# A 3008-point Fourier filter and an ELU layer on one core: the transform's last products as two 64x128 tiles instead of four 64x64 tiles

## The chip, the core and the metric

The kernel runs on one core of a Trainium2 chip. The metric is device time in microseconds (us) of one execution; lower is better. A change of 0.2%, about 5 us here, is about the smallest that a measurement of this kernel can tell from none.

## The reference

```python
X = np.fft.rfft(x, axis=1)                 # x: (8, 3008, 256) float32
Y = X * (filt_r + 1j * filt_i)[None]       # filters: (1505, 256)
y = np.fft.irfft(Y, n=3008, axis=1)
h = y.reshape(24064, 256) @ w_in           # (256, 2048)
g = np.where(h > 0.0, h, np.exp(np.minimum(h, 0.0)) - 1.0)
out = g @ w_out                            # (2048, 256)
```

Everything is float32.

## The kernel before, in words

The sequence length is split as 3008 = 47 x 64, and the transform, the filter and the inverse transform are done as small matrix products over these factors, one of the eight batches after the other. The result of the inverse's first factor goes through DRAM (the tensor `yds`) and is read back by `y_read` as a tile `t` of 128 partitions by 4 indices by 256 channels. The third factor, which this change touches, is the last of the transform: `n_unit(b, m)` multiplies `t` with a table `w` of cosines and sines (`tn_read`), four indices `i` of the 24 at a time, so there are six units a batch (m = 0 to 5). The first unit of the first batch is made by another function, `n_first`, with full 128x128 tiles of weights and 128 (or 64) moving columns (line 575). That leaves 47 units of `n_unit`.

In one unit the contraction runs over 64 rows. The rows 0 to 63 hold one half of the terms and 64 to 127 the other (`HALVES`); their products go to two PSUM banks, `pse` and `pso`. The stationary operand (the weights that are loaded into TensorE) is a slice of the data `t`; the moving operand is the table, 64 columns wide, or 32 for the index i = 0. The channels are the output rows: 256 of them, as `dh` = 0, 1 of 128 each, and each 128 as `o` = 0, 64 of 64 each. ScalarE then copies both banks into `y` (line 558), VectorE makes sums from them (`n_sums`, lines 592 to 603), and the two layers follow.

The layers are done by `up_steps` (the product with `w_in`, line 624, into the banks `phs`, `pha`, `phd`) and `down_steps` (the product with `w_out`, line 707, into `po`), with the seven products of Strassen's scheme in Winograd's form for each 2 by 2 block. These are full 128x128 tiles of weights with 256 (for m = 0: 224) moving columns. ScalarE makes the ELU's exponentials (lines 635, 641, 642), VectorE the sums and maxima (lines 632, 646, 682 to 686).

Nothing is scheduled by a tool: the order is written by hand. The work is a list of 192 items (batch, m, quarter of the hidden layer), here called quads, 24 to a batch. In each quad the steps of "up" and "down" are interleaved one by one, and a plan (`at(quad, place, function, ...)`) puts the transform's pieces at five places in a quad. Each batch's transform is spread over the quads of the batch before it. Each engine works through its instructions in this order. While the first quads run, the weights are also converted from 64-bit to 32-bit numbers (the `w_...` functions).

A float32 product appears in the profile as two pairs of LDWEIGHTS (the load of weights, shown as PEld) and MATMUL (shown as PE). A unit of `n_unit` has 32 products, so 64 such pairs; they stand in groups of four tiles that occupy different quarters of the array at one time (two halves of the rows by two halves of the columns), 16 groups to a unit.

Of the kernel before, what the change touches and what calls it, by code (L numbers as in the profile page):

```python
# [26 lines left out]
P = 128  # L27
# [14 lines left out]
HALVES = slice(0, 64), slice(64, 128)  # L42
# [91 lines left out]
def order(m):  # L134

    return (1, 2, 3, 0) if m == 0 else tuple(range(4 * m, 4 * m + 4))
# [3 lines left out]
def kernel(  # L140
# [9 lines left out]
    nc = tc.nc  # L150
# [49 lines left out]
    def bank(name, shape=(P, 2, D)):  # L200
        i = banks.pop(0)
        return i, psM.tile(list(shape), FP32, tag="m%d" % i, name=name)
# [337 lines left out]
    def half(m):  # L540

        return 224 if m == 0 else 256

    def n_unit(b, m):
        t, w, h = t4s.pop((b, m)), tns.pop((b, m)), half(m)
        ps = [bank(n) for n in ("pse", "pso")]
        for q, i in enumerate(order(m)):
            n = 32 if i == 0 else 64
            for dh in range(2):
                for o in (0, 64):  # L550
                    for (_, p), r in reversed(tuple(zip(ps, HALVES))):
                        nc.tensor.matmul(p[o:o + 64, dh, ds(64 * q, n)], t[r, i - 4 * m, ds(dh * P + o, 64)],  # L552
                                         w[r, i - 4 * m, 0:n], start=True, stop=True)
        eo = []
        yset = ysets[(6 * b + m + (6 * b + m > 1)) % 2]
        for (k, p), scale, y in zip(ps, (1.0, -2.0), yset):
            y = y[:, :, 0:h]
            nc.scalar.activation(out=y, in_=p[:, :, 0:h], func=AXT.Copy, scale=scale)
            banks.append(k)
            eo.append(y)  # L560
        s = yset[2]
        ys[b, m] = dict(zip((1, 3, 5, 4, 6, 2, 7), [t[:, i] for t in eo for i in range(2)] + [s[:, i, 0:h] for i in range(3)]))
# [315 lines left out]
    with tc.manual_schedule():  # L878


        with tc.tile_pool(name="boot", bufs=1) as bp:
# [122 lines left out]
            for k in range(11):  # L1004
                nc.tensor.matmul(warm, w_in[0][:, 0, 0, :], w_in[0][:, 0:2].rearrange("p a b c -> p (a b c)"),
                                 start=True, stop=True)
# [13 lines left out]
        def at(quad, place, fn, *a):  # L1020
# [5 lines left out]
                 (0, 0, w_split, 8), (0, 0, x_load, 1, 2),  # L1026
                 (0, 3, w_float, 11, 1), (0, 3, w_sums, 5, nc.gpsimd), (0, 3, w_join, 7, 0), (0, 3, w_join, 9, 1), (0, 3, w_fetch, 15, nc.sync),
                 (1, 2, w_float, 8, 1, 0), (1, 2, y_write_first, 5, 8, 24), (1, 2, w_mult, 7, nc.vector), (1, 2, w_float, 8, 2), (1, 2, x_unit, 1, 0, 0), (1, 2, x_unit, 1, 0, 1), (1, 2, n_unit, 0, 1),
                 (1, 4, w_float, 11, 2),
                 (1, 0, w_join, 8, 0), (1, 0, x_unit, 1, 1, 0), (1, 0, x_unit, 1, 1, 1), (1, 0, f_arrange, 1, 1), (1, 0, n_sums, 0, 1, 0, 1), (1, 0, w_sums, 7, nc.gpsimd),  # L1030
# [19 lines left out]
                 (5, 0, w_join, 15, 0), (5, 0, w_join, 14, 0), (5, 0, y_read, 0, 3), (5, 0, w_join, 15, 1),  # L1050
                 (5, 3, w_mult, 15, nc.gpsimd),
                 (5, 1, c_last, 0, 0), (5, 1, w_mult, 14, nc.gpsimd), (5, 1, w_sums, 15, nc.gpsimd), (5, 1, n_unit, 0, 2),
                 (6, 2, n_sums, 0, 2, 0, 1),
                 (6, 0, n_sums, 0, 2, 2),
                 (8, 0, n_unit, 0, 3),
                 (9, 1, n_sums, 0, 3))
        for quad, place, fn, *a in early:
# [7 lines left out]
        for b in range(B):  # L1065
            t = (b - 1) * PER
            if b > 0:
                for c in range(NXC):
# [9 lines left out]
                    if nb < B:  # L1078
                        q, p = (((2, 1), (8, 1), (11, 1)) if b == 1 else XL)[c // 2]
# [92 lines left out]
```

## Time and profile before

| | before |
|---|---|
| median of 3 runs | 2549.34 us (2549.11 to 2549.7) |
| profiled execution: its own time, its span | 2550.1 us, 2548.3 us |
| TensorE products (PE) busy | 2518.0 us (99%) |
| TensorE weight loads (PEld) busy | 2151.5 us (84%) |
| VectorE (DVE) busy | 2099.9 us (82%) |
| ScalarE (ACT) busy | 1524.9 us (60%) |
| granted TensorE clock, mean | 0.997 |

The profile is of one execution; its own time is 0.03% above the median. Durations of matmuls are modelled and overlap each other, so the sum of their busy times is not the time that they take of the span; the distance from one start to the next is. In the shapes, "64*64 64x64" means weights of 64 rows and 64 columns, and 64 rows by 64 columns of moving data.

### The profile page before, as it was taken

The page shows a single profiled execution, that of the slowest core. Times are in us where ns is not written, and L with a number is a line of the kernel's source. Part 1 is how long each engine was busy: PE and PEld are TensorE (multiplying, and loading weights), DVE is VectorE, ACT ScalarE, POOL GpSimd, SP SyncE. Part 2 cuts the span into 40 slices and gives each one's busy share as a digit, 9 for nine tenths or more (in the row PEclk, how much of TensorE's full clock was granted, in tenths as well). Part 3 has the DMA queues.
Part 4 walks back from the last instruction along what each step waited for, and adds up shares of the span by engine and source line. Part 5 has one row for each costly group of instructions (what it writes and reads, how often), then busy time and mean ns, then how long its engine had stood idle before and what let it go on. Part 6 is the DMA issues. An engine that isn't in the chain of part 4 may idle for free.

```text
span 2548.3 us, 45119 instructions
## 1 busy us (share of the span) xinstructions
PE 2518.0 (99%) x17326; PEld 2151.5 (84%) x17326; DVE 2099.9 (82%) x3654; ACT 1524.9 (60%) x2702; POOL 170.4 (7%) x242
## 2 busy tenths in 40 slices
PE   8899999999999999999999999999999999999998
PEld 5688889888898888988889888888889888898887
DVE  5998888888888888788887888878898788876766
ACT  6666556655566555665566655666656665555554
POOL 3431000000000000000000000000000010000000
PEclk9999999999999999999999999999999999999999
DMA  8645214423243321433225331343314332110010
GB/s 210 197 121 124 58 41 105 108 58 71 46 104 91 70 64 42 124 81 77 45 52 139 76 67 34 78 120 80 69 21 98 86 67 59 42 40 19 20 27 17
DMA packets 227958, 194.07 MB, mean 76 GB/s; under 512 B 125493, under 2 KB 208407, under 8 KB 225007
## 3 DMA queue, kind: packets, MB, share of 16 engines
q1 hardware_dynamic: 216815, 167.35, 27.2%
q0 software_dynamic: 9776, 23.58, 4.5%
q8 instruction: 136, 2.23, 0.4%
q14 instruction: 79, 0.65, 0.1%
q10 hardware_dynamic: 1152, 0.26, 0.1%
HBM read 119.24 MB, written 74.97 MB: 76 GB/s over the span
## 4 chain that ended last, share of the span: by engine, by line
PE 93%; DVE 4%; ACT 1%; issue 1%; DMA 1%; POOL 0%; SPq 0%; DVEq 0%; POOLq 0%; ACTq 0%
PE po L707 44%; PE phs L624 25%; PE phd L624 12%; PE pha L624 6%; PE pso L552 2%; PE pf L451 1%; PE pv L517 1%; PE psa L272 1%; DVE g L646 0%; PE psa L324 0%; DVE g L632 0%; PE pse L552 0%; DMA t<-tf_t 0%; PE po L385 0%; PE po L343 0%
## 5 line engine op out<-in xcount | busy, mean ns | idle before, releaser
L707 PE MATMUL po<-g,wo 128*128 128x256 f32 (+1 forms) x5376 | 1317.5, 377 | 0.0
L707 PEld LDWEIGHTS po<-g,wo 128*128 128x128 f32 x5376 | 1012.9, 190 | 162.8 <-issue 49.2
L635 ACT ACTIVATE g<-phs 128x512 f32<-128x512 f32 (+1 forms) x576 | 338.9, 588 | 726.5 <-PE phs L624 726.5
L624 PE MATMUL phs<-y,wi 128*128 128x256 f32 (+1 forms) x2288 | 581.0, 376 | 2.1 <-ACT g L635 1.6
L642 ACT ACTIVATE e<-e 128x512 f32<-128x512 f32 (+1 forms) x768 | 477.2, 621 | 24.3
L624 PEld LDWEIGHTS phs<-y,wi 128*128 128x128 f32 x2288 | 429.2, 190 | 59.8 <-ACT g L635 4.4
L632 DVE TENSOR_TENSOR g<-phd,g 128x512 f32<-128x512 f32 (+1 forms) x384 | 259.4, 675 | 223.4 <-ACT e L642 148.8
L646 DVE SCALAR_TENSOR_TENSOR g<-e,g 128x512 f32<-128x512 f32 (+1 forms) x576 | 391.4, 679 | 0.2
L641 ACT ACTIVATE e<-g 128x512 f32<-128x512 f32 (+1 forms) x576 | 353.1, 613 | 54.0 <-DVE g L632 44.3
L646 DVE SCALAR_TENSOR_TENSOR g<-e,phs 128x512 f32<-128x512 f32 (+1 forms) x192 | 129.8, 676 | 130.5 <-ACT e L642 130.4
L624 PE MATMUL phs<-ys,wi 128*128 128x256 f32 (+1 forms) x784 | 198.0, 375 | 7.0 <-ACT g L635 5.0
L624 PE MATMUL phd<-y,wi 128*128 128x256 f32 (+1 forms) x768 | 194.1, 375 | 5.1 <-DVE g L632 5.1
L624 PE MATMUL phd<-ys,wi 128*128 128x256 f32 (+1 forms) x768 | 193.9, 375 | 1.1 <-DVE g L632 1.0
L624 PE MATMUL pha<-ys,wi 128*128 128x256 f32 (+1 forms) x752 | 190.0, 375 | 0.0
L641 ACT ACTIVATE e<-phs 128x512 f32<-128x512 f32 (+1 forms) x192 | 113.0, 589 | 114.7 <-PE phs L624 114.6
L624 PEld LDWEIGHTS phs<-ys,wi 128*128 128x128 f32 x784 | 148.0, 190 | 26.0 <-ACT g L635 6.2
L624 PEld LDWEIGHTS phd<-y,wi 128*128 128x128 f32 x768 | 145.5, 190 | 23.0 <-DVE g L632 6.7
L624 PEld LDWEIGHTS phd<-ys,wi 128*128 128x128 f32 x768 | 145.7, 190 | 18.3 <-DVE g L632 1.8
L624 PEld LDWEIGHTS pha<-ys,wi 128*128 128x128 f32 x752 | 142.8, 190 | 16.5
L632 DVE TENSOR_TENSOR g<-pha,g 128x512 f32<-128x512 f32 (+1 forms) x192 | 129.1, 673 | 22.9 <-PE pha L624 13.2
L683 DVE TENSOR_TENSOR g<-g,g 128x512 f32<-128x512 f32 (+1 forms) x192 | 132.0, 687 | 6.7
L686 DVE TENSOR_TENSOR g<-g,g 128x512 f32<-128x512 f32 (+1 forms) x192 | 131.1, 683 | 6.7
(200 smaller groups left out, 2100.5 us busy)
## 6 DMA issues: line engine op xcount, KB each, us to landing
t<-yd SPq DMA_DIRECT2D x94, 256.0 KB
z<-t SPq DMA_DIRECT2D x84, 256.0 KB
fall<-fp POOLq DMA_DIRECT2D x112, 192.0 KB, 5.1
t<-z SPq DMA_DIRECT2D x112, 192.0 KB
yd<-t SPq DMA_DIRECT2D x112, 192.0 KB
out_dram<-o SPq DMA_DIRECT2D x632, 32.0 KB
xc<-in_x_dram SPq DMA_DIRECT2D x84, 128.0 KB
xc<-in_x_dram SPq DMA_DIRECT2D x161, 64.0 KB
```

Source lines behind the costliest of these rows:

```text
L272: nc.tensor.matmul(p[32 * o:32 * o + 32, j, :], w[r, ts(o, 32)], t[r, o % 2, o // 2, :], start=True, stop=True, tile_position=(32 * a, 32 ...
L451: nc.tensor.matmul(pf[p][1][32 * a:32 * a + 32, js, :], fb[r, v, :], t2[r, js, a, :], start=True, stop=True, tile_position=(32 * p, 32 * a))
L552: nc.tensor.matmul(p[o:o + 64, dh, ds(64 * q, n)], t[r, i - 4 * m, ds(dh * P + o, 64)], w[r, i - 4 * m, 0:n], start=True, stop=True)
L624: nc.tensor.matmul(ps[:, a, 0:h], w_in[q][:, COMBO[n], a, :], y[n], start=start and a == 0, stop=True, skip_group_check=True)
L632: nc.vector.tensor_tensor(out=g[o], in0=i0, in1=i1, op=ALU.add)
L635: nc.scalar.activation(out=g[o], in_=i0, func=AXT.Copy)
L641: nc.scalar.activation(out=e, in_=src, func=AXT.Relu, scale=-1.0)
L642: nc.scalar.activation(out=e, in_=e, func=AXT.Exp, scale=-1.0)
L646: nc.vector.scalar_tensor_tensor(out=g[n], in0=es[n], scalar=1.0, in1=src, op0=ALU.subtract, op1=ALU.max)
L683: nc.vector.tensor_tensor(out=b12, in0=b22, in1=b12, op=ALU.subtract)
L686: nc.vector.tensor_tensor(out=g["t4"], in0=g["b21"], in1=g["t2"], op=ALU.subtract)
L707: nc.tensor.matmul(po[i][:, u, 0:h], w_out[q][:, COMBO[n], a, :], g[n][:, a, :], start=begin and a == 0 and n in (1, 3, 6, 4), stop=True, ...
```

## The change

The loop over `o` goes. One product takes all 128 channels of a `dh` as its output rows, with weights of 64 rows by 128 columns, and writes all 128 partitions of its bank. Two such tiles, one on the rows 0 to 63 and one on 64 to 127, stand side by side where four tiles of 64 by 64 stood. A unit has 16 products instead of 32, 32 pairs of load and matmul instead of 64, and still 16 groups. The values and their places in PSUM stay as they were, and so does every other instruction.

```diff
         for q, i in enumerate(order(m)):
             n = 32 if i == 0 else 64
             for dh in range(2):
-                for o in (0, 64):
-                    for (_, p), r in reversed(tuple(zip(ps, HALVES))):
-                        nc.tensor.matmul(p[o:o + 64, dh, ds(64 * q, n)], t[r, i - 4 * m, ds(dh * P + o, 64)],
-                                         w[r, i - 4 * m, 0:n], start=True, stop=True)
+                for (_, p), r in reversed(tuple(zip(ps, HALVES))):
+                    nc.tensor.matmul(p[:, dh, ds(64 * q, n)], t[r, i - 4 * m, ts(dh, P)], w[r, i - 4 * m, 0:n],
+                                     start=True, stop=True)
```

## Prediction

> **What bounds the kernel now.** I read the busy times and the chain of waits on the page first, and then the busy times by stage.
>
> ```profile
> span 2548.3 us, 45119 instructions
> ...
> PE 2518.0 (99%) x17326; PEld 2151.5 (84%) x17326; DVE 2099.9 (82%) x3654; ACT 1524.9 (60%) x2702; POOL 170.4 (7%) x242
> ...
> PE 93%; DVE 4%; ACT 1%; issue 1%; DMA 1%; POOL 0%; SPq 0%; DVEq 0%; POOLq 0%; ACTq 0%
> ```
>
> ```profile
> 84.00:212.00 128.00, 116.59 (x818) 99.52 (x817) 120.98 (x191) 83.24 (x151) 47.42 (x49) 0.99 0.53 140
> 212.00:2442.00 2230.00, 2229.77 (x15545) 1921.29 (x15544) 1856.92 (x3247) 1334.44 (x2359) 89.12 (x139) 1.00 0.30 70
> ```
>
> The columns of the busy times by stage are the stretch, its length, and the busy us of PE, PEld, DVE, ACT and POOL, then the granted clock. From 212 us to 2442 us TensorE is busy for 2229.77 of 2230 us, at full clock: nothing makes it wait, and what is added to or taken from its stream there is added to or taken from the time, one for one. Between 84 and 212 us, while weights are still converted, VectorE is busy for 120.98 of 128 us and TensorE has 11.4 us of gaps. A busy share of 99% doesn't say what TensorE is busy with: a product that waits for its weights counts as busy too. So the next views are the groups by shape, and one unit in order of time.
>
> ```profile
> L552 PEld LDWEIGHTS pso<-tn,t 64*64 64x64 f32 x1504 | 47.8, 134 | 15.2 <-issue 12.8 <-DVE g L685 2.3
> L272 PEld LDWEIGHTS psa<-xc,ta 32*32 32x32 f32 x1152 | 14.5, 103 | 9.0 <-issue 5.3
> L575 PEld LDWEIGHTS psn<-t,t4f 128*128 128x128 f32 x16 | 1.9, 191 | 0.9 <-DMA t4f<-yd 0.9
> ```
>
> Behind the bar stand the busy us and the mean ns of one load. A load grows with its columns: 103 ns for 32, 134 ns for 64, 191 ns for 128; the step from 64 to 128 is 57 ns. Now one unit of m = 0, first its loads, then its last products, which have 32 moving columns (start in us, duration):
>
> ```profile
> 1002.10 0.13 PEld L552 LDWEIGHTS pso<-tn,t 64*64 64x64 f32 x1 [0.33 <-DVE g L685]
> ...
> 1002.97 0.14 PEld L552 LDWEIGHTS pso<-tn,t 64*64 64x64 f32 x1
> 1002.98 0.14 PEld L552 LDWEIGHTS pse<-tn,t 64*64 64x64 f32 x1
> 1002.99 0.14 PEld L552 LDWEIGHTS pso<-tn,t 64*64 64x64 f32 x1
> 1002.99 0.14 PEld L552 LDWEIGHTS pse<-tn,t 64*64 64x64 f32 x1
> 1003.17 0.94 PEld L707 LDWEIGHTS po<-g,wo 128*128 128x128 f32 x5
> ```
>
> ```profile
> 1002.88 0.22 PE L552 MATMUL pso<-tn,t 64*64 64x32 f32 x1
> ...
> 1002.94 0.22 PE L552 MATMUL pso<-tn,t 64*64 64x32 f32 x1
> ...
> 1003.00 0.22 PE L552 MATMUL pso<-tn,t 64*64 64x32 f32 x1
> ```
>
> ```profile
> 69.85 1.86 PEld L575 LDWEIGHTS psn<-t,t4f 128*128 128x128 f32 x16 [0.94 <-DMA t4f<-yd]
> 70.40 0.75 PEld L575 LDWEIGHTS psn<-t,t4f 128*128 128x128 f32 x6
> ```
>
> The sixteenth group of loads starts 0.87 us after the first, so a group takes 0.87 / 15 = 0.058 us. Its four loads start within 20 ns and run at the same time. A stream of 64 columns takes a quarter of the 0.216 us that lies between the starts of 256-wide products, 0.054 us, and would almost explain the 0.058. The 32-wide products tell it apart: with half the stream they still start every 0.06 us. So the load of 64 columns sets the rhythm, and the stream lies beneath it. The last two lines, from `n_first`, are the nearest thing to what the change makes: loads of 128 columns with short streams behind them. Sixteen take 1.86 us, the last one 0.19 of it, so one starts every 1.67 / 15 = 0.111 us; six in the middle every (0.75 - 0.19) / 5 = 0.112 us. Four of the sixteen products have only 64 moving columns; by their streams alone, the fifteen steps would be twelve of 0.107 and three of 0.054 us, 1.45 us. They took 1.67: loads set the rhythm here too, about twice as long for twice the columns.
>
> **The change part by part.**
>
> *Removed:* half of the products of line 552, 47 x 16 = 752, that is, 1504 pairs of load and matmul. Their issue costs nothing now: the four loads of a group start 7 ns apart, and the next group's first follows about 40 ns after the fourth. What they free is not on the path.
>
> *Made longer:* each of the 16 groups of a unit now loads 128 columns instead of 64 on each half of the rows. No trace row has a load of 64 rows by 128 columns. Loads of 24x32 and 32x32 both take 103 ns, those of 48x64 133 ns against 134 ns for 64x64; fewer rows don't make a load shorter, so I take the 128x128 rhythm: 0.112 - 0.058 = 0.054 us for each group. The ends: 0.049 us (the step of a load 0.107 us, without the gap of 5 ns that the rows show) and 0.057 us (the difference of the mean durations, 191 - 134). One unit costs 16 x 0.054 = 0.864 us more. The two streams of a pair, 0.054 us, hide beneath the next load; without that cover a group would take 0.054 us more, 38 us once again; the rows of line 575, where the streams are as long or longer and still lie beneath the loads, speak against that.
>
> *Units on the path:* 44 of the 47 units start after 212 us (the first at 246 us): 44 x 0.864 = 38.0 us. The other three, at 84, 159 and 191 us, stand where TensorE has gaps of 0.7 to 3 us behind them, left by VectorE. Their 2.6 us are swallowed there, or they delay VectorE's next input and pass through. Between 0 and 2.6 I take half, 1.3 us, because in that stretch the chain of waits goes through both engines.
>
> *Entry and exit:* the first small load starts 0.31 us after the start of the last 256-wide product, where 0.216 is usual: 0.09 us lost for emptying the array. Behind the last load the next 128x128 load comes 0.18 us later, 0.07 more than the 0.11 from load to load where loads set the rhythm. Tiles that divide only the rows don't occur in the trace. The 32x32 tiles of lines 451 and 517 are entered at the same 0.31 us as the 64x64 ones, so I leave both as they are: 0. The ends: both vanish, 44 x 0.16 = -7.0 us; or emptying takes twice as long, 44 x 0.09 = +4.0 us.
>
> *Behind it:* ScalarE's copies of a unit (line 558), VectorE's sums and the next "up" steps start 0.86 us later, like TensorE's own next steps, which wait in order behind the unit. ACT has 40% idle, DVE 17% in that stage, so both keep the pace of a slower TensorE. Nothing on ACT, DVE, POOL or SP is added, taken away or moved: their streams are the same, instruction for instruction. No queue or transfer is touched.
>
> *Sum:* 38.0 + 1.3 = 39.3 us. On the profiled execution, 2550.1 + 39.3 = 2589.4 us; on the median, 0.8 us below it, 2549.3 + 39.3 = 2588.6 us, or +1.5%.
>
> **The rivals.**
>
> *First: the pair is bound by its streams, and having fewer tiles saves launches (not slower).* It holds if a load of 64x128 fits into 0.058 us, say because a tile that keeps all columns is loaded by another way than one that divides them. Then the group shrinks from 0.058 to its stream of 0.054 us: 752 x 0.004 = 3 us, 2546 us. If entry and exit vanish too, 7 us more: 2539 us. For it: no row has this shape, and four launches at 7 ns become two. Against it: the 32-wide groups that don't shrink, and the 0.112 us steps. The Trainium skill, "TensorE: Matmul & The Clock Gate", section "Measured speedup vs the span model", is on this rival's side: it gives a pack of tiles the time of one matmul plus about 4 ns for each further tile, with no term for the columns of the loads. By that rule two tiles fewer would save some 8 ns a group, an estimated 6 us in all. The trace speaks against the rule in this place: 64 and 32 moving columns give the same rhythm.
>
> *Second: the two loads of a pair don't overlap (much slower).* If two 128-column loads share a path that four 64-column loads did not need, a group takes 2 x 0.112 us: 0.166 more, 16 x 0.166 = 2.66 us a unit, 117 us for 44 units, with half of the other three 2549.3 + 117 + 4 = 2670 us. Against it: now tiles on the same columns and different rows (`pso` at 1002.97, `pse` at 1002.98) load at the same time, and the change keeps that.
>
> *Third: the program that is built still has four tiles,* and the time is 2549. The built program has 752 products fewer on TensorE, each with 128 output rows, so this is next to excluded.
>
> **How the numbers follow.** The forecast case gets 0.86: both its rhythms are measured in this trace, and what is unmeasured is only that the 128-column step holds on 64 rows. The first rival gets 0.08, of which 0.05 ends within 0.2% (5 us, about what a measurement of this kernel can tell from no change) and 0.03 below it; the second 0.05; the third 0.01. So faster 0.03, same 0.06, slower 0.91. The range is that of the forecast case with the ends of its terms. Low: the shorter step, 16 x 44 x 0.049 + 1.3 = 35.8 us, with entry and exit gone, -7.0: 28.8 us, 2578. High: the longer step in all 47 units, 47 x 16 x 0.057 = 42.9 us, or the middle sum with the doubled emptying, 39.3 + 4.0 = 43.3 us: 2593. The rivals' 0.14 lies outside.
>
> **What would show it.** Right: loads of line 551 of 64x128, half as many, near 190 ns each, in pairs every 0.112 us; a unit's loads spread over 15 x 0.112 = 1.68 us instead of 0.87; the start of the next 128x128 load 0.18 us behind the last pair; the stretch from 212 us on still without a gap of TensorE and 38 us longer; DVE and ACT busy for the same us. Wrong: pairs every 0.058 us (first rival), or single loads every 0.112 us (second); entries of other than 0.31 us; a growth between 84 and 212 us that is not between 0 and 2.6 us.

## The result, and the profile after

The changed kernel took 2589.26 us, the median of five runs (2586.39 to 2591.72), beside 2549.34 us before (2549.03 to 2549.88 in five runs): 1.0155 times the time, 95% interval 1.0143 to 1.0168. Measured once more beside other kernels, it took 2586.63 us against 2549.78 us, 1.0146 (1.0132 to 1.0160). So it is slower by 37 to 40 us; 39.3 were forecast, and the traces say below that some 37.6 is the better number.

The profiled execution took 2586.39 us. First the page's busy times and chain, then the busy times by stage (stretch, length, busy us of PE, PEld, DVE, ACT, POOL, granted clock):

```profile
span 2584.6 us, 42111 instructions
...
PE 2556.6 (99%) x15822; PEld 2191.7 (85%) x15822; DVE 2099.8 (81%) x3654; ACT 1529.7 (59%) x2702; POOL 170.4 (7%) x242
...
PE 94%; DVE 2%; DMA 2%; ACT 1%; issue 0%; SPq 0%; DVEq 0%; ACTq 0%
```

```profile
84.00:214.00 130.00, 119.93 (x749) 102.49 (x746) 121.50 (x193) 83.39 (x151) 47.49 (x49) 0.99 0.54 141
214.00:2480.00 2266.00, 2265.78 (x14157) 1957.89 (x14156) 1854.12 (x3243) 1339.62 (x2360) 89.00 (x139) 1.00 0.30 69
```

TensorE has 1504 pairs of load and product fewer and is busy longer. In the long stretch it is as full as before (2265.78 of 2266 us), and VectorE does the same work in more time. The page alone can't say more: "99%" stood there before too. The group by shape (busy us, mean ns) and the same unit as before the change, in order of time (start, duration), say it:

```profile
L551 PEld LDWEIGHTS pso<-tn,t 64*128 64x128 f32 x752 | 87.3, 188 | 15.2 <-issue 12.8 <-DVE g L684 2.3
```

```profile
1013.21 0.18 PEld L551 LDWEIGHTS pso<-tn,t 64*128 64x128 f32 x1 [0.33 <-DVE g L684]
1013.22 0.18 PEld L551 LDWEIGHTS pse<-tn,t 64*128 64x128 f32 x1
1013.32 0.19 PEld L551 LDWEIGHTS pso<-tn,t 64*128 64x128 f32 x1
...
1014.77 0.19 PEld L551 LDWEIGHTS pso<-tn,t 64*128 64x128 f32 x1
1014.78 0.19 PEld L551 LDWEIGHTS pse<-tn,t 64*128 64x128 f32 x1
1014.88 0.19 PEld L551 LDWEIGHTS pso<-tn,t 64*128 64x128 f32 x1
1014.89 0.19 PEld L551 LDWEIGHTS pse<-tn,t 64*128 64x128 f32 x1
1015.12 0.51 PEld L706 LDWEIGHTS po<-g,wo 128*128 128x128 f32 x3
```

The two loads of a pair start 7 ns apart and run together. The sixteenth pair starts 1014.88 - 1013.21 = 1.67 us after the first, so a pair follows every 1.67 / 15 = 0.111 us where a group of four followed every 0.058. The last pairs serve products with 32 moving columns and keep the same rhythm. The load is 188 ns long, like that of 128 full rows (190).

What this is worth is read between two places of the trace that are the same in both programs: the first product of the fourth unit, where TensorE's gaps end, and that of the last unit. Before, then after:

```profile
246.19 0.27 PE L552 MATMUL pso<-tn,t 64*64 64x64 f32 x1
...
2442.31 0.27 PE L552 MATMUL pso<-tn,t 64*64 64x64 f32 x1
```

```profile
245.54 0.32 PE L551 MATMUL pso<-tn,t 64*128 64x64 f32 x1
...
2477.79 0.32 PE L551 MATMUL pso<-tn,t 64*128 64x64 f32 x1
```

The distance was 2196.12 us and is 2232.25 us: 36.13 us over 43 units, 0.840 us each, and with the last unit 44 x 0.840 = 37.0 us. The stretch ahead of the fourth unit is 0.65 us shorter in this execution, so the span grew by 36.13 + 0.84 - 0.65 = 36.3 us. What the three units ahead of it add is read among the experiments.

### The profile page after: what moved, and what is told of

Its sections match the earlier page's. It is cut to its first block, busy times and chain, and to the rows that moved or that the text cites. A ratio compares the mean times of both kernels' runs of the same rounds, so it can differ in the third digit from the quotient of the medians.

```text
span 2584.6 us, 42111 instructions
## 1 busy us (share of the span) xinstructions
PE 2556.6 (99%) x15822; PEld 2191.7 (85%) x15822; DVE 2099.8 (81%) x3654; ACT 1529.7 (59%) x2702; POOL 170.4 (7%) x242
## 4 chain that ended last, share of the span: by engine, by line
PE 94%; DVE 2%; DMA 2%; ACT 1%; issue 0%; SPq 0%; DVEq 0%; ACTq 0%
PE po L706 43%; PE phs L623 25%; PE phd L623 12%; PE pha L623 6%; PE pso L551 3%; PE pf L451 1%; PE pv L517 1%; PE psa L272 1%; PE po L385 0%; DMA x<-in_x_dram 0%; PE psr L385 0%; DVE g L645 0%; DMA fall<-in_moe_w_out_dram 0%; DVE g L631 0%; DMA xc<-in_x_dram 0%
```

## The experiments

Three questions were left. Do load and stream of neighbouring groups overlap, or add up (0.054 + 0.054 us and a few ns would also make 0.112)? Is it the columns of a load that count, or that only two tiles stand abreast? And do the first three units cost anything?

**The changed kernel again, and the change in a part of the units.** The last two have this edit, with `> 3` for the 44 late units and `< 4` for the three early ones:

```diff
+                if 6 * b + m > 3:      # early only: < 4
+                    ... the two 64x128 tiles
+                else:
+                    ... the four 64x64 tiles
```

> The changed kernel once more, beside the kernels below on the same chip. In its first profile each of the 47 units took 0.84 us longer, and the 44 units behind 212 us gave 44 x 0.84 = 37.0 us; the first three were swallowed. Theory (every unit costs the same in every run, and what differs from run to run is the start): the five times lie between 2586 and 2592 as before, and in the profile the distance from the fourth unit to the last is again 2232.3 us. Rival (the units or the products between them vary): that distance differs by some us.

> Two 64x128 tiles in the 44 units from the fourth on, four 64x64 tiles in the three units of the start. Theory (the first three are swallowed by TensorE's gaps): the same time as with all 47 changed, 2549.3 + 37.0 = 2586.3 us, up to the run-to-run spread of the changed kernel. Rival (the three pass through): 2.5 us less than all 47 changed.

> Two 64x128 tiles in the first three units alone. Theory (swallowed): 2549.3 us, and in the trace the gaps of TensorE behind these units are shorter by 0.84 us each. The prediction's middle value: 2550.6. Rival (passes through): 2551.8 us. If the spread of some us that the changed kernel shows comes from these three units, it shows here too; if from the other 44, here the spread is under 1 us.

Against 2549.78 us for the kernel before on the same chip, all units: 2586.63 us; the late ones: 2587.12 us (2585.59 to 2588.38); the early ones: 2549.71 us, ratio 1.0000 (0.9991 to 1.0009). By the times, the 44 late units carry it, and the early three cost less than can be told: the interval reaches to 2.3 us, so it speaks against the full 2.5 us and no more. The times with the early units alone spread from 2547.52 to 2552.24 us, as widely as those before, so the spread comes neither from them nor from the other 44.

The starts of the units in the traces say more. From the second unit to the third it is 32.04 us before and with the late units alone, and 32.62 to 32.63 us in the changed kernel, in the changed kernel again and with the early units alone. So 0.58 of the second unit's 0.84 us pass through. From the third unit to the fourth it is 54.97 to 54.98 us in all five: the third unit is swallowed.

These are the products of TensorE that wait behind the second and the third unit, with the gap ahead of them in brackets, first before and then with the early units alone:

```profile
179.99 1.02 PE L624 MATMUL phs<-ys,wi 128*128 128x224 f32 x4 [0.79 <-ACT g L635]
197.28 1.13 PE L624 MATMUL phd<-y,wi 128*128 128x256 f32 x4 [1.47 <-DVE g L632]
```

```profile
182.18 1.02 PE L629 MATMUL phs<-ys,wi 128*128 128x224 f32 x4 [0.86 <-ACT g L640]
199.46 1.13 PE L629 MATMUL phd<-y,wi 128*128 128x256 f32 x4 [0.63 <-DVE g L637]
```

The gap behind the third unit, which VectorE ends, shrinks by the unit's 0.84 us. The gap behind the second, which ScalarE ends, does not shrink. In the changed kernel the products behind the third unit stand 0.84 us later relative to those of before; behind VectorE's next sum, 5 us on, they are 0.85 us earlier again. What the first unit costs stays open, because stretches of half the clock lie between it and the second unit, in other places in each execution. The expectation that all three are swallowed was wrong for the second.

The distance from the fourth unit to the last was 2232.24 us in the changed kernel again, 2232.23 with the late units alone, and 2196.11 with the early ones alone: the same to 0.02 us as in the first profiles. The rival of the first expectation, units that vary, falls.

**Longer streams in both kernels.** Every product takes 128 moving columns. The added columns are the table's next index, and they overwrite each other in the banks, so the outputs of these two kernels are other values; the number of products and groups stays:

```diff
-  p[..., dh, ds(64 * q, n)], ..., w[r, i - 4 * m, 0:n]
+  p[..., dh, ds(64 * min(q, 2), 128)], ..., w[r, ds(min(i - 4 * m, 2), 2), :]
```

> The changed kernel with 128 moving columns in every product instead of 64 or 32 (the table's next index taken along, so the outputs of the third factor are others): streams of 107 ns, loads as in the changed kernel. Theory (a group takes the longer of load and stream, and the 128-column load of 0.107 us plus 5 ns sets it): twice the work for the same 0.112 us a group, only the last stream of a unit is 0.05 us longer: the distance from the fourth unit to the last 2232.2 + 43 x 0.05 = 2234.5 us, the time about 2589 us. Rival (load and stream of the next group add up): 0.054 us more a group, 2232.2 + 43 x 0.85 = 2269 us, time 2624 us.

> The kernel before, four 64x64 tiles, with 128 moving columns in every product (outputs of the third factor are others): loads of 64 columns, streams of 107 ns. Theory: now the stream sets the group, 0.107 to 0.112 us, so the unit is as long as that of the changed kernel, from the other side: distance from the fourth unit to the last 2232 to 2235 us, time 2585 to 2589 us. Rival (load and stream add up): 0.054 + 0.107 us a group and more, 2196.1 + 43 x 16 x 0.1 = 2265 us.

The changed kernel with doubled streams took 2589.72 us beside 2550.26 us (ratio 1.0156, 1.0141 to 1.0171); distance 2234.94 us, 2.69 more than with short streams, 0.06 us a unit. The kernel before with doubled streams took 2586.72 us (1.0143, 1.0126 to 1.0160); distance 2231.36 us. Loads in the last groups of a unit, first two tiles, then four:

```profile
1051.24 0.19 PEld L551 LDWEIGHTS pso<-tn,t 64*128 64x128 f32 x1
...
1051.35 0.19 PEld L551 LDWEIGHTS pso<-tn,t 64*128 64x128 f32 x1
...
1051.46 0.19 PEld L551 LDWEIGHTS pso<-tn,t 64*128 64x128 f32 x1
```

```profile
1051.48 0.13 PEld L552 LDWEIGHTS pso<-tn,t 64*64 64x64 f32 x1
1051.48 0.13 PEld L552 LDWEIGHTS pse<-tn,t 64*64 64x64 f32 x1
1051.49 0.13 PEld L552 LDWEIGHTS pso<-tn,t 64*64 64x64 f32 x1
1051.50 0.13 PEld L552 LDWEIGHTS pse<-tn,t 64*64 64x64 f32 x1
1051.59 0.13 PEld L552 LDWEIGHTS pso<-tn,t 64*64 64x64 f32 x1
```

With two tiles the rhythm is 0.11 us as without the doubling: twice the multiplying for almost nothing, because the stream lies beneath the load. With four tiles it went from 0.058 to 0.11 us: now the stream sets it. Load and stream don't add up. The two kernels reach the same time from opposite sides.

**Two tiles abreast, with 64 columns each.** The loop over `o` moves outside those over `q` and `dh`:

```diff
+        for o in (0, 64):
             for q, i in enumerate(order(m)):
                 n = 32 if i == 0 else 64
                 for dh in range(2):
-                    for o in (0, 64):
```

> The same 32 products a unit as before, reordered: all with o = 0 first, then all with o = 64. So a group is two tiles of 64x64 on the same columns, two abreast as in the changed kernel, but with 64-column loads; there are 32 groups a unit. Theory (the columns of a load set the rhythm, not how many tiles stand abreast): 0.058 us a group, 32 x 0.058 = 1.86 us a unit, 0.93 us more than before: distance from the fourth unit to the last 2196.1 + 43 x 0.93 = 2236 us, time about 2590 us. Rival (two row tiles alone are slower than four tiles, whatever their columns: 0.112 us a group): 3.58 us a unit, 2196.1 + 43 x 2.66 = 2310 us, time 2666 us.

It took 2583.29 us beside 2550.26 us (1.0131, 1.0116 to 1.0146), distance 2228.23 us. The loads of a unit, in the middle of it:

```profile
1047.33 0.14 PEld L552 LDWEIGHTS pso<-tn,t 64*64 64x64 f32 x1
...
1047.38 0.14 PEld L552 LDWEIGHTS pso<-tn,t 64*64 64x64 f32 x1
...
1047.44 0.14 PEld L552 LDWEIGHTS pso<-tn,t 64*64 64x64 f32 x1
1047.45 0.14 PEld L552 LDWEIGHTS pse<-tn,t 64*64 64x64 f32 x1
1047.45 0.13 PEld L552 LDWEIGHTS pso<-tn,t 64*64 64x64 f32 x1
...
1047.50 0.14 PEld L552 LDWEIGHTS pso<-tn,t 64*64 64x64 f32 x2
```

Two tiles abreast with 64 columns keep the rhythm of 0.058 us. The rival with 0.112 us for any pair falls. The number of tiles doesn't make the changed kernel's 0.111 us, and its streams don't either, by the experiment before; what is left are the columns of a load. A unit grew by 32.11 / 43 = 0.75 us, not by the 0.93 that was expected: at 1047.45 the first pair with `o` = 64 starts 10 ns behind a pair with `o` = 0, and the next ones run beside each other too ("x2"). Three groups of the second half are pulled ahead onto the free columns and cost nothing, 3 x 0.058 = 0.17 us.

**Eight tiles of 64x32.** More tiles, shorter loads:

```diff
-                for o in (0, 64):
+                for o in (0, 32, 64, 96):
                     for (_, p), r in reversed(tuple(zip(ps, HALVES))):
-                        nc.tensor.matmul(p[o:o + 64, ...], t[r, i - 4 * m, ds(dh * P + o, 64)], ...
+                        nc.tensor.matmul(p[o:o + 32, ...], t[r, i - 4 * m, ds(dh * P + o, 32)], ...
```

> Eight tiles of 64 rows by 32 columns in a group in place of four of 64x64: half the load, the same streams, twice the launches. Theory (a group takes the longer of its load and its stream, with a few ns between): the load falls to about 30 ns and lies beneath the stream of 54 ns, a group takes 54 to 58 ns as before, the first load of a unit is 0.03 us shorter: 2545 to 2549.3 us. Rival (load and stream add up, as 54 + 54 ns also gives the 112 ns of the changed kernel with a few ns): the group shrinks by 27 ns, 752 x 0.027 = 20 us, 2529 us. Rival (launches bind, 7 ns for each load and product): sixteen in a group, some 0.11 us a group, 2549.3 + 752 x 0.05 = 2587 us or more.

It took 2571.13 us against 2549.78 us (1.0079, 1.0066 to 1.0093): slower, where the theory said 0 to 4 us faster. The theory lacked a term.

```profile
1044.72 0.11 PEld L552 LDWEIGHTS pso<-tn,t 64*32 64x32 f32 x1
1044.72 0.11 PEld L552 LDWEIGHTS pse<-tn,t 64*32 64x32 f32 x1
...
1044.77 0.18 PEld L552 LDWEIGHTS pso<-tn,t 64*32 64x32 f32 x2
1044.91 0.10 PEld L552 LDWEIGHTS pse<-tn,t 64*32 64x32 f32 x1
...
1045.10 0.11 PEld L552 LDWEIGHTS pse<-tn,t 64*32 64x32 f32 x2
1045.12 0.11 PEld L552 LDWEIGHTS pso<-tn,t 64*32 64x32 f32 x2
1045.13 0.11 PEld L552 LDWEIGHTS pse<-tn,t 64*32 64x32 f32 x2
1045.15 0.12 PEld L552 LDWEIGHTS pso<-tn,t 64*32 64x32 f32 x2
```

At first the tiles start 7 ns apart and a group takes 0.056 us; its stream (0.054 us) and eight starts 7 ns apart (0.056 us) would both give that. From 1044.77 to 1044.91 us little starts, and after that two loads start every 16 to 17 ns: 8 x 8.2 = 0.066 us a group. The stream is shorter than that, and so is even the 0.058 us of a load with twice the columns, so the issue of the instructions probably sets it; no run tests it apart.

A unit got 0.32 us longer, 47 x 0.32 = 15 us of the 21. Most of this is not the rhythm. From every eighth load to the next, three of the fifteen steps of this unit take 0.18, 0.13 and 0.13 us instead of 0.067, one behind each 32 loads: 0.23 us. Why TensorE halts there is open. In the profiled execution it also stood still once: two products of line 707 start 2.3 us apart (at 1942 us), and the granted clock was 0.5 behind that, from 1945 to 1948 us. The distance from the fourth unit to the last is 2214.1 us, 18.0 more than before; 43 x 0.32 = 13.8 us of that are the units, and the halt and the clock make up some 4 us. The rest of the 21 us was not pursued. Rival "launches" came nearest, but it took 7 ns for each load and each product where a pair of them has 8 ns, and it did not have the halts.

## Why the prediction was right

*The bound.* Right. TensorE was full from 212 us on, every us that a unit grew went into the time, and VectorE, ScalarE and the queues did the same work as before.

*The rhythm of a group, 0.112 for 0.058 us.* Right, and it carried the forecast. It came from a row of another function, 16 loads at 70 us, with 128 rows in place of 64; 64 rows made no difference (188 and 190 ns, 0.111 and 0.112 us).

*One unit, 0.864 us.* Measured 0.840. The fifteen steps from the first group to the sixteenth grew from 0.87 to 1.67 us, 0.80; the longer last load shows behind them, where the next full tile comes 0.23 us after it instead of 0.18 (0.26 instead of 0.20 in most units), 0.05. (The prediction counted this in its 16 groups, yet said that the 0.18 would stay: that sign was wrong.) From these 0.85 go 0.01, since the last of two tiles starts 7 ns behind the first and the last of four 20 ns. That is the saving of the first rival: it exists, once a unit and not once a group. The other 0.01 of the difference is rounding, 0.054 for 0.0534.

*Units on the path.* 44, as said. *The early three, 1.3 us:* the second costs 0.58 us, the third nothing, and the first can't be read. The middle of two ends was taken without a look at each gap. VectorE's 121 busy us of 128 were a good guide to the third, where VectorE ends the gap, and not to the second.

*Entry and exit at 0:* right. The first small load comes 0.31 us behind the start of the last 256-wide product for 64x128 tiles too, and what the exit grew by is the sixteenth load, which the sum already held.

*Sum.* 39.3 us forecast; 37.0 + 0.6 = 37.6 us by the traces, without the first unit. Both terms of the forecast were a little high, the late units by 1.0 us and the early ones by up to 0.7. The first median, 39.9 us over before, lies nearer to the forecast than the mechanism does, which is luck; the second, 36.9 us, lies nearer to the traces. By the profiles, executions differ by some us in their start (last section); the runs without a profile don't show where the 3 us between the two medians lie.

*The rivals.* The first, streams set the pair, would have left 0.058 us; shown wrong by the trace and by the doubled streams. The rule of the Trainium skill ("TensorE: Matmul & The Clock Gate", section "Measured speedup vs the span model") is one matmul plus about 4 ns for each further tile. With the stream put in for the matmul, it gives an estimated 0.107 + 3 x 0.004 = 0.119 us for four tiles with 128 moving columns, where 0.109 was measured, and 0.054 + 0.004 = 0.058 us for the changed kernel's two, where 0.111 was measured: it is near where the stream is the longest part and fails where the load is. The second, loads in series, is refuted by `pso` and `pse` at 1013.21 and 1013.22 us. The third by the 64x128 loads themselves.

## What to carry to other kernels

In the shapes run here, a group of small float32 tiles takes the longer of two: the load of one tile's columns (0.058 us for 64, 0.111 for 128) and its stream (0.054 us for 64 moving columns, 0.109 measured for 128). A third, the issue of all its tiles (some 8 ns each in a long row), is inferred from the eight tiles alone. Four 64x64 tiles with 64 moving columns have 0.058, 0.054 and 0.033 us: they are near balance. Fewer and wider tiles break it by the load; eight narrow ones were slower too, by issue and halts. So look for the load's rhythm in any row of the profile with the same columns, and never take half the instructions for half the time.

## What the runs showed of the hardware beside this

The times of one kernel spread over some 5 us (before: 2546.40 to 2551.72 us in fifteen runs). As far as the profiles show, this does not lie in the long stretch: from the fourth unit to the last, executions with the same units agree to 0.02 us. The one that lost time there is that of the eight tiles, some 4 us at 1942 us. The difference lies in the start. In the nine profiles the fourth unit began at 244.99, 245.54, 246.13, 246.19, 246.97, 247.63, 248.34, 248.37 and 250.49 us, and the granted clock of the first 240 us was 0.99, 0.99, 0.97, 0.98, 0.98, 0.97, 0.97, 0.96 and 0.96 in the same order: but for one, the lower the clock, the later the unit. For a change of some us, the distance between two marks in the steady part of the traces is the sharper measure.
